# Blocks 5 and 6 of the first MLP computed as a pair with seven products, and attention's last product in fp32

## The chip, the cores and the metric

One core of a Trainium2 chip runs the whole program. Its engines are TensorE (PE; PEld is its weight load), VectorE (DVE), ScalarE (ACT), GpSimd (POOL) and SyncE (SP), which here issues nearly all DMAs. The metric is the device time of one execution in microseconds. Three runs of the kernel before gave 1582.0, 1582.98 and 1583.49; the median is 1582.98.

## What is computed

```python
# attention: q, k, v are (8, 8, 576, 64)
q_s = softmax(q, axis=-1)                       # over the 64 entries of a head
k_s = softmax(k, axis=2)                        # over the 576 positions
kv  = einsum('bhsd,bhse->bhde', k_s, v)         # 64 x 64 for each head
x   = einsum('bhsd,bhde->bhse', q_s, kv)        # 8 x 8 x 576 x 64
x   = x.transpose(0, 2, 1, 3).reshape(4608, 512)
# first MLP: w_in 512 x 2048, w_out 2048 x 512
h = x @ w_in;   x = (h * clip(h + 3, 0, 6) / 6) @ w_out
# second MLP, same shapes
h = x @ w2_in;  return (h / (1 + exp(-h))) @ w2_out
```

## The kernel before

The 4608 tokens are nine blocks of 512 (0 to 8). Every product of an MLP is made of three passes in fp32r (high by high, high by low, low by high), so each operand is held as a high and a low part: a copy on ACT makes the high part, a subtraction on DVE the low part.

**A block by itself** has 16 slices of 128 hidden columns. A slice has 12 matmuls of 512 columns into one bank `h` (`mm1`, L561), the gate on ACT and DVE (`Gate`, L574 to L592), and 12 matmuls into four banks `y` (`mm2`, L633; L635 in the second MLP). A slice is a step. Before, blocks 0 to 6 of the first MLP and block 0 of the second are done so.

**A pair of blocks** is one pass of `second_mlp`: the 2 x 2 scheme with seven products in place of eight. Its first half ("inner", L1345) has 8 rounds of seven products, its second half ("outer", L1504) seven products of 8 rounds; each of the 112 has 6 matmuls. The operands are sums of quarters. Those of the weights lie in DRAM (`ws`, second index: which of the two matrices; first index: which MLP) and are fetched into a ring of six buffers; those of the tokens are made during the pass before (`x_ahead`). `PASSES` lists the passes as (MLP - 1, first block): before it is (1, 1), (0, 7), (1, 3), (1, 5), (1, 7). An inner half also carries the transposes of the results of the pass before (`turn_blocks`), an outer half the splits of the gates (L1450 on ACT, L1332 on DVE; L1332 is a helper that records every `add`).

**Attention** works in 36 units, one for each block and pair of heads. A unit makes `kv` (`kv_mm`, L397, ten fp32 matmuls of 65 columns), turns the normalized q (early units by TensorE, later ones through DRAM: `q_blocks`, `q_store`, `q_load`) and multiplies both (`x_mm`, L515). Before, `x_mm` takes three fp32r products of split operands: `kv_upper`, `kv_lower`, `q_upper`, `q_lower` make the parts. A block of 512 tokens can lie in two batches, and then the product is made in two pieces.

**The weights** arrive in a packed form. `Conv` unpacks a slice (ACT L120, L124; DVE L132, L139, L143). Those of the first MLP stay in SBUF for the single blocks; those of the second are unpacked during the single blocks, split (`Split`, ACT L223, DVE L226), summed in place on POOL (`sums_in_place`, L194), and stored to `ws`. For the pair (0, 7) the same was done with the first MLP's weights (`Resident`).

**The order** of `first_block` (to the end of block 0) and `middle` (the other single blocks) is made by `Plan`: jobs with an engine, an estimated duration, a key (the step that they belong to, shifted by the tables `LATE`, `WORK`, `FETCH`, `UNIT`, `CONV`, `RAW`), dependencies, and buffers taken and given. It plays them against its estimates and writes each engine's instructions in the resulting order; on the chip each engine works through its list strictly in that order. `second_mlp` is ordered by a list of events in units of one product (6 matmuls). SP's list is in order as well: a DMA that waits for its producer holds all behind it.

Of the kernel before, what the change touches and what calls it, by code (L numbers as in the profile page):

```python
# [28 lines left out]
def efficient_attention_then_two_mlps(  # L29
# [24 lines left out]
    NCL = NB - 2  # L54
    FAR = 4
    PASSES = ((1, 1), (0, NCL)) + tuple((1, j) for j in range(3, NB, 2))
# [17 lines left out]
    kvt = [const.tile([P, 2, P], F32R, name=f"kv{i}") for i in range(KVS)]  # L74
# [8 lines left out]
    ws = dram.tile([2, 2, 4 * NF, P, DM], F32, name="ws")  # L83
    xq = dram.tile([NB - FAR, NC, P, BLK], F32, name="xq")
# [118 lines left out]
    def store_parts(ph, o, i, flat, names):  # L203
        for h, name in enumerate(names):
            if name != "A21" or ph:
                nc.sync.dma_start(
                    ws[ph, o, slot(o, i, name)].rearrange("p (a d) -> p a d", a=2),
                    f32(flat)[:, :, h * HALF : (h + 1) * HALF],
                )

    class Split:
# [13 lines left out]
        def lower(self):  # L225
            nc.vector.tensor_tensor(out=self.lo, in0=self.src(), in1=f32(self.hi), op=ALU.subtract)  # L226
# [21 lines left out]
    class Resident:  # L248


        def __init__(self, i, o):
            self.i, self.o = i, o
            self.split = [
                Split(0, o, i, lambda n=n: self.t[:, n], [INTO[x] for x in NAMES[o][n]], False)
                for n in range(2)
            ]
            self.total = [
                lambda m=m: sums_in_place(o, [self.t[:, n] for n in range(2)])[m]() for m in range(4)
            ]

        def flat(self, n):
            f = 2 * self.i + n
            return wo[0, f] if self.o else wi[0, f].rearrange("p a c f -> p a (c f)")

        def whole(self, n):
            if n == 0:
                self.t = raw.tile([P, 2, DM], F32, tag="raw", name="w1_sum")
            w = self.flat(n)
# [140 lines left out]
    def kv_upper(u):  # L409
        pk, rs, t = live["pk", u], live["rs", u], kvt[u % KVS]  # L410
        kv[divmod(u, NP)] = t
        for h in range(2):
            d = slice(h * D, (h + 1) * D)
            nc.scalar.activation(t[d, 0, d], pk[d, 0:D], AF.Copy, scale=rs[d])

    def kv_lower(u):
        pk, rs, t = live.pop(("pk", u)), live.pop(("rs", u)), kvt[u % KVS]
        for h in range(2):
            d = slice(h * D, (h + 1) * D)
            nc.vector.scalar_tensor_tensor(  # L420
                out=t[d, 1, d], in0=pk[d, 0:D], scalar=rs[d], in1=f32(t[d, 0, d]),
                op0=ALU.mult, op1=ALU.subtract,
            )
# [60 lines left out]
    def q_load(u):  # L484
        t = tmp.tile([P, NCH * P], F32, tag="t2k", name="qt")
# [7 lines left out]
    def q_upper(u):  # L493
        qT = att.tile([P, 2, NCH, P], F32R, tag="qT", bufs=1, name="qT")
        nc.scalar.copy(qT[:, 0].rearrange("p i n -> p (i n)"), live["pq", u])
        live["qT", u] = qT

    def q_lower(u):
        qT = live["qT", u]
        nc.vector.tensor_tensor(  # L500
            out=qT[:, 1].rearrange("p i n -> p (i n)"),
            in0=live.pop(("pq", u)),
            in1=f32(qT[:, 0]).rearrange("p i n -> p (i n)"),
            op=ALU.subtract,
        )

    def x_mm(u):
        j, pr = divmod(u, NP)
        qT = live.pop(("qT", u))
        px = a_psum(None)  # L510
        pv = px.rearrange("p (i n) -> p i n", i=NCH)
        for p0, n, b, _ in parts(j):
            w = kv[b, pr]
            for n_, (a, c) in enumerate(((0, 0), (0, 1), (1, 0))):
                nc.tensor.matmul(  # L515
                    pv[:, :, p0 : p0 + n], w[:, a, :], qT[:, c, :, p0 : p0 + n],
                    start=(n_ == 0 and p0 == 0), stop=(n_ == 2), skip_group_check=True,
                )
        live["px", u] = px

    def x_upper(u):
        j, pr = divmod(u, NP)
        if j >= FAR:
            t = live["xq", u] = tmp.tile([P, BLK], F32, tag="t2k", name="xq")
# [208 lines left out]
    class Plan:  # L733
# [84 lines left out]
    LATE = (0, 0, 1.5, 1, 1, 1, 0, 0, -1.5, 0.5, 0.5, 0.5, 0, 0, 0, 0, 0, 0, 0, 0, -1, 2, 0, 0, 3,  # L818
        1.5, 0.5, 2.5)
    WORK = (-2, 0, 0, 0, 0.5, -0.5, 0, -1.5, 0.5, 2.5, 2, 2, 0, 4, 2, 2)  # L820
    FETCH = (2, 0, 0, 0, 0, -0.5, -0.5, -1, -1, -0.5, -2, -1)

    UNIT = (0, -1.5, -1.5, 1.5, 2, 2, 2, 2, 4)
    CONV = (0, 1.5, 1.5, 1.5, 1, 1, 1.5, 1.5, 1, 0.5, 0, -0.5, -1, 0.5, 0, 0, -0.5, 0, -1, -1, 0,
        0.5, 0, -0.5, -1, 2, 0, 1, 0.5, 0.5, 0, 1)
    RAW = (-0.5, 0, 0, 0, 2, 0, 1, 0.5, -2, -2, -2, 0, 0, 0, 0, 0, 0, 0, -2, -1, -1, 1, 0, 0, 0, 0,
        2, 0, -0.5, -2, -2, -2)


    DIRECT_X = ()  # L830
    DIRECT_G = ()
# [888 lines left out]
```

## Time and profile before

| | |
|---|---|
| median of three runs | 1582.98 us |
| profiled execution | 1584.67 us |
| its span, first to last instruction | 1583.0 us |
| PE, PEld, DVE, ACT, POOL busy | 98%, 81%, 72%, 49%, 31% |
| HBM read, written | 247.20 MB, 94.11 MB |
| SP's queue, share of the 16 DMA engines | 69.3% |

The span falls into four parts: up to about 31 us loads and the first units of attention; then the single blocks of the first MLP to 726 us; five passes to 1490.5 us; block 0 of the second MLP to the end. A matmul's record covers its way through the engine, and the records overlap, so a PE busy of 98% isn't work at full rate. The pace is read from the starts: from one run of matmuls to the next.

### The profile page before, as it was taken

How to read it: one execution, taken by the hardware profiler on the slowest of the kernel's cores; microseconds unless marked ns; L12 is line 12 of the kernel's file. 1: busy time of each engine (PE TensorE's matmuls, PEld its weight loads, DVE VectorE, ACT ScalarE, POOL GpSimd, SP SyncE). 2: the span in 40 equal slices, each digit the busy share in tenths (PEclk: the TensorE clock that was granted, in tenths of full speed). 3: DMA queues.
4: the chain of work that ended last, by engine and by line, in shares of the span. 5: the costliest groups of instructions: out<-in, count | busy, mean ns of one | idle time of the engine just before them, and what ended most of it. 6: DMA issues, size and time to landing. Idle time of an engine off the chain costs nothing.

```text
span 1583.0 us, 22655 instructions
## 1 busy us (share of the span) xinstructions
PE 1555.3 (98%) x7388; PEld 1274.9 (81%) x7388; DVE 1146.3 (72%) x1888; ACT 775.1 (49%) x1390; POOL 490.8 (31%) x443
## 2 busy tenths in 40 slices
PE   5999999999999999999999999999999999999998
PEld 3777888887878888888888888888888888888887
DVE  7898567777777787675689569946986697676632
ACT  5787345555555555454355336523543464345322
POOL 3234233334243344632223233223223422440000
PEclk9999999999999999999999999999999999999999
DMA  9914977777777775857566786765667875879840
GB/s 271 332 37 131 321 214 209 204 232 223 238 206 214 228 236 191 255 173 243 197 217 224 206 230 222 256 211 193 234 206 216 222 252 191 225 229 365 259 127 27
DMA packets 391206, 342.85 MB, mean 217 GB/s; under 512 B 184880, under 2 KB 297520, under 8 KB 391088
## 3 DMA queue, kind: packets, MB, share of 16 engines
q1 hardware_dynamic: 389040, 340.32, 69.3%
q8 instruction: 59, 0.97, 0.2%
q10 hardware_dynamic: 2048, 1.08, 0.2%
q14 instruction: 59, 0.48, 0.1%
HBM read 247.20 MB, written 94.11 MB: 216 GB/s over the span
## 4 chain that ended last, share of the span: by engine, by line
PE 93%; DVE 3%; DMA 1%; ACT 1%; issue 1%; SPq 0%; POOL 0%; ACTq 0%; DVEq 0%; POOLq 0%
PE pb L1345 24%; PE pb L1504 24%; PE h L561 21%; PE y L633 17%; PE y L635 3%; PE pa L515 2%; PE pa L397 1%; DVE fa L139 1%; DMA yd<-o 0%; DVE fa L143 0%; DVE fa L132 0%; DVE h L598 0%; DMA wi_early<-in_moe_w_in_dram 0%; DMA ws<-fa 0%; PE pa L368 0%
## 5 line engine op out<-in xcount | busy, mean ns | idle before, releaser
L561 PE MATMUL h<-x,wi 128*128 128x512 f32 x1536 | 382.2, 396 | 1.8 <-ACT g L609 1.4
L1345 PE MATMUL pb<-xo,ring 128*128 128x512 f32 x1680 | 382.6, 389 | 0.0
L1504 PE MATMUL pb<-gsp,ring 128*128 128x512 f32 x1680 | 382.4, 389 | 0.0
L1345 PEld LDWEIGHTS pb<-xo,ring 128*128 128x128 f32 x1680 | 315.3, 188 | 65.5
L1504 PEld LDWEIGHTS pb<-gsp,ring 128*128 128x128 f32 x1680 | 315.3, 188 | 65.5
L561 PEld LDWEIGHTS h<-x,wi 128*128 128x128 f32 x1536 | 285.4, 189 | 63.7 <-ACT g L609 2.2
L633 PE MATMUL y<-g,wo 128*128 128x512 f32 x1344 | 324.6, 391 | 0.7 <-DVE o L652 0.7
L633 PEld LDWEIGHTS y<-g,wo 128*128 128x128 f32 x1344 | 251.0, 188 | 53.7 <-DVE o L652 1.1
L1332 DVE TENSOR_TENSOR gsp<-g,gsp 128x512 fp32r<-128x512 f32 x240 | 182.5, 780 | 25.4 <-ACT gsp L1450 24.7
L1450 ACT CAST gsp<-g 128x512 fp32r<-128x512 f32 x240 | 143.7, 622 | 106.7 <-PE pb L1504 89.4
L574 ACT ACTIVATE r<-h 128x512 f32<-128x512 f32 x112 | 67.0, 598 | 172.4 <-PE h L561 169.9
L598 DVE SCALAR_TENSOR_TENSOR h<-r,h 128x512 f32<-128x512 f32 x112 | 77.5, 692 | 82.6 <-ACT r L574 82.0
L1332 POOL TENSOR_TENSOR xst<-xst 128x512 f32<-128x512 f32 x32 | 71.5, 2235 | 167.5 <-DVE xo L1332 87.1
L1332 DVE TENSOR_TENSOR g<-r,pb 128x512 f32<-128x512 f32 x96 | 65.7, 684 | 54.6 <-ACT r L1359 54.1
L1359 ACT ACTIVATE r<-pb 128x512 f32<-128x512 f32 x96 | 57.1, 594 | 97.2 <-DVE pb L1332 72.8
L1332 POOL TENSOR_TENSOR g<-g 128x512 f32<-128x512 f32 x40 | 53.5, 1338 | 138.2 <-DVE g L1332 113.0
L1332 POOL TENSOR_TENSOR s<-U,s 128x512 f32<-128x512 f32 x32 | 42.3, 1321 | 174.0 <-DVE U L1332 174.0
L589 ACT CAST g<-h 128x512 fp32r<-128x512 f32 x112 | 65.5, 585 | 46.2 <-DVE h L598 38.5
L436 POOL TENSOR_TENSOR qe<-qraw,qm 128x512 f32<-128x512 f32 x34 | 40.2, 1181 | 152.3 <-DVE qz L478 130.2
L592 DVE TENSOR_TENSOR g<-h,g 128x512 fp32r<-128x512 f32 x96 | 66.0, 688 | 21.1 <-ACT g L589 19.8
L1332 DVE TENSOR_TENSOR U<-pb,s 128x512 f32<-128x512 f32 x80 | 55.0, 688 | 17.4 <-PE pb L1345 12.5
L194 POOL TENSOR_TENSOR fa<-fa 128x256 f32<-128x256 f32 x64 | 49.5, 774 | 55.9 <-DVE sp L226 47.8
(161 smaller groups left out, 1778.7 us busy)
## 6 DMA issues: line engine op xcount, KB each, us to landing
ring<-ws SPq DMA_DIRECT2D x280, 512.0 KB, 3.9
ws<-sp SPq DMA_DIRECT2D x256, 128.0 KB, 2.2
wi_early<-in_moe_w_in_dram SPq DMA_DIRECT2D x16, 512.0 KB, 8.7
wo_early<-in_moe_w_out_dram SPq DMA_DIRECT2D x16, 512.0 KB, 8.9
wi_raw<-in_moe_w_in_dram SPq DMA_DIRECT2D x16, 512.0 KB, 5.0
ws<-w_sum SPq DMA_DIRECT2D x64, 128.0 KB, 2.2
ws<-fa SPq DMA_DIRECT2D x64, 128.0 KB, 1.8
wo_raw<-in_moe_w_out_dram SPq DMA_DIRECT2D x16, 512.0 KB, 4.3
```

The source lines that it names most:

```text
L194: lambda to=to, x=x, y=y, op=op: nc.gpsimd.tensor_tensor(out=at[to], in0=at[x], in1=at[y], op=op)
L561: nc.tensor.matmul(h, w[:, a, c, :], x[:, e, c, :], start=(c == 0 and n == 0), stop=(c == NC - 1 and n == 2),)
L574: nc.scalar.activation(self.r, self.h, AF.Relu, bias=3.0)
L589: nc.scalar.copy(self.g[:, 0], self.r)
L592: nc.vector.tensor_tensor(out=self.g[:, 1], in0=self.r, in1=f32(self.g[:, 0]), op=ALU.subtract)
L598: nc.vector.scalar_tensor_tensor(out=self.h, in0=self.r, scalar=6.0, in1=self.h, op0=ALU.min, op1=ALU.mult)
L633: nc.tensor.matmul(y[c], w[:, a, cs], g[:, e, :], start=st, stop=sp)
L1332: (eng or nc.vector).tensor_tensor(out=out, in0=a, in1=b, op=how)
L1345: nc.tensor.matmul(to, ws_[:, a], e[:, c], start=p in ("P1", "P6", "P5") and c == 0 and m == 0, stop=c == 1 and m == 2, skip_group_check=True,
L1359: nc.scalar.activation(r, d[b, n, key], AF.Sigmoid)
L1450: nc.scalar.copy(t[0], source(p, i))
L1504: nc.tensor.matmul(d[b, p][m], w[:, a, m * P : (m + 1) * P], t[e], start=new and i == 0 and k == 0, stop=i == NPR - 1 and k == 2, skip_gro ...
```

## The change

Two more blocks, 5 and 6, leave the single blocks (`NCL` is `NB - 4`) and become the pass (0, 5). The passes are now (1, 1), (1, 3), (0, 5), (0, 7), (1, 5), (1, 7). The stores of the first MLP's plain quarters move from `middle` into `first_block` (`store_first`); in `middle` only the fp32 sum of high and low part is made (POOL) and stored whole (`wf`), and its sums of quarters and splits are made in the inner halves of the first three passes (`first_forms`). `x_mm` is one fp32 product. Some `Split.lower` go to POOL (`ASIDE_P`), four `x_lower` and one gate of `first_block` go from TensorE and ACT to DVE (`DIRECT_X`, `DIRECT_G`), a sum in the inner halves of the second and third pass goes from POOL to DVE (`c22`). The last three units load q and make `x_mm` in the first pass. The tables of the planner are new.

```diff
-    NCL = NB - 2
+    NCL = NB - 4
-    PASSES = ((1, 1), (0, NCL)) + tuple((1, j) for j in range(3, NB, 2))
+    PASSES = ((1, 1), (1, 3), (0, 5), (0, 7), (1, 5), (1, 7))
...
         def whole(self, n):
+            f = 2 * self.i + n
             if n == 0:
                 self.t = raw.tile([P, 2, DM], F32, tag="raw", name="w1_sum")
...
-        def store(self, n):
-            store_parts(0, self.o, self.i, self.flat(n), NAMES[self.o][n])
+        def store(self):
+            nc.sync.dma_start(wf[self.o, self.i], self.t)
...
-    def kv_lower(u):
...
-            nc.scalar.activation(t[d, 0, d], pk[d, 0:D], AF.Copy, scale=rs[d])
+            nc.scalar.activation(t[d, d], pk[d, 0:D], AF.Copy, scale=rs[d])
...
-    def q_lower(u):
...
+    def x_mm(u, pool=lambda: a_psum(None)):
...
         for p0, n, b, _ in parts(j):
-            w = kv[b, pr]
-            for n_, (a, c) in enumerate(((0, 0), (0, 1), (1, 0))):
-                nc.tensor.matmul(
-                    pv[:, :, p0 : p0 + n], w[:, a, :], qT[:, c, :, p0 : p0 + n],
-                    start=(n_ == 0 and p0 == 0), stop=(n_ == 2), skip_group_check=True,
-                )
+            nc.tensor.matmul(
+                pv[:, :, p0 : p0 + n], kv[b, pr], qt[:, :, p0 : p0 + n],
+                start=p0 == 0, stop=True, skip_group_check=True,
+            )
...
-            begin[j * NP + pr] = 3 * pr if j == 1 else NF - 3 + int(3.3 * n) + LATE[n]
+            begin[j * NP + pr] = 3 * pr if j == 1 else NF - 3 + 2.3 * n + LATE[n]
...
-            at = NF + 5.5 * k + 6 + WORK[k]
+            at = NF + 3.7 * k + 4 + WORK[k]
...
-                    nc.gpsimd if b else nc.vector,
+                    nc.gpsimd if b > 2 else nc.vector,
...
+        def first_forms(k, t):
+            o, i = divmod(k, NPR)
+            st = {}
...
+            def high(n):
...
+                nc.scalar.copy(st[n][:, 0], st["t"][n])
+            def low(n):
+                add(st[n][:, 1], st["t"][n], f32(st[n][:, 0]), ALU.subtract)
+            def store(n):
+                for h, x in enumerate(NAMES[o][n]):
+                    nc.sync.dma_start(
+                        ws[0, o, slot(o, i, INTO[x])].rearrange("p (a d) -> p a d", a=2),
+                        f32(st[n])[:, :, h * HALF : (h + 1) * HALF],
+                    )
+            when(t, load)
+            for m in range(4):
+                when(t + 5.8 + 0.6 * m, lambda m=m: sums_in_place(o, st["t"])[m]())
+            for n in range(2):
+                when(t + 12.0 + 0.8 * n, lambda n=n: high(n))
+                when(t + 12.6 + 0.8 * n, lambda n=n: low(n))
+                when(t + 14.0 + 0.8 * n, lambda n=n: store(n))
...
+            for n, k in enumerate(range(5 * b, min(5 * b + 5 + b // 2, 2 * NPR)) if b < 3 else ()):
+                first_forms(k, t0 + (9.0 if b == 0 else 1.2) + (6.6 if b != 1 else 7.2) * n)
...
+        for n, u in enumerate(range(LATER, NB * NP)):
...
+            when(0.1 + 0.1 * n, lambda u=u, to=q_to: q_load(u, to))
+            when(4.97 + n, lambda u=u: x_mm(u, bank))
+            when(6.05 + n, lambda u=u, to=x_to: (x_upper(u, to), x_store(u)))
```

What moves is shown at three places. The first is ACT's list from its first copy for attention on, a few instructions into the program (`qT` or `qt` is the turned q, `x` the block's operand, `fa` and `fr` the unpacking of weights). Before:

```order
L495 CAST qT<-pa 128x512
L414 ACTIVATE kv_94<-pk,small 64x64 x2
L446 ACTIVATE qe<-qe 128x512
L414 ACTIVATE kv_93<-pk,small 64x64 x2
L120 ACTIVATE fa<-wi_early 128x512
L124 ACTIVATE fr<-wi_early 128x512
L495 CAST qT<-pa 128x512
L529 CAST x<-pa 128x512
```

and of the changed kernel:

```order
L479 COPY qt<-pa 128x512
L430 ACTIVATE qe<-qe 128x512
L407 ACTIVATE kv_94<-pk,small 64x64 x2
L502 CAST x<-pa 128x512
L430 ACTIVATE qe<-qe 128x512
L522 CAST x<-pa 128x512
L121 ACTIVATE fa<-wi_early 128x512
L125 ACTIVATE fr<-wi_early 128x512
```

Both copies of the first unit's result `x` and one more exponential now stand ahead of the first weight's unpacking.

The second is SP's list in the middle of the single blocks (`ws` holds the weights' quarters and sums, `zd` and `qt` the way of q through DRAM, `xq` the results of attention for later blocks). Before:

```order
L232 DMA ws<-sp 128x256
L232 DMA ws<-w_sum 128x256
L105 DMA wi_raw<-in_moe_w_in_dram 128x4x256
L482 DMA zd<-qz 128x512
L676 DMA xq<-xq 128x512
L322 DMA qraw<-in_q_dram 80x2x256
L322 DMA qraw<-in_q_dram 48x2x256
L232 DMA ws<-sp 128x256 x4
L488 DMA qt<-zd 32x16x32 x4
```

and of the changed kernel:

```order
L255 DMA wf<-w_sum 128x1024
L466 DMA zd<-qz 128x512
L225 DMA ws<-sp 128x256 x4
L315 DMA qraw<-in_q_dram 96x2x256
L315 DMA qraw<-in_q_dram 32x2x256
L100 DMA wo_raw<-in_moe_w_out_dram 128x1024 x2
L472 DMA qt<-zd 32x16x32 x4
```

The first MLP's weights leave by one DMA in place of eight small ones and three of plain quarters; the rest of the list stays and stands closer. In all of `middle` SP issues 635 DMAs (256 `ws<-sp` and `ws<-fa`, 96 `qt<-zd`, 69 `vbuf`, 214 others), before 821 (384 to `ws` from `sp`, `fa` and `w_sum`, 108, 66, 263 others).

The third is TensorE's list at the start of the first pass (`y` is the last single block's output, `pb` the pass's banks). Before:

```order
L633 MATMUL y_6943<-g,wo 128x512
L633 MATMUL y_6944<-g,wo 128x512
L1345 MATMUL pb<-xo,ring 128x512 x318
L1504 MATMUL pb<-gsp,ring 128x512 x6
L1345 MATMUL pb<-xo,ring 128x512 x6
L1504 MATMUL pb<-gsp,ring 128x512 x330
```

and of the changed kernel:

```order
L1326 MATMUL pb<-xo,ring 128x512 x18
L488 MATMUL pb<-qt,kv_97 128x512
L1326 MATMUL pb<-xo,ring 128x512 x6
L488 MATMUL pb<-qt,kv_93 128x512
L1326 MATMUL pb<-xo,ring 128x512 x6
L488 MATMUL pb<-qt,kv_94 128x512
L1326 MATMUL pb<-xo,ring 128x512 x288
L1485 MATMUL pb<-gsp,ring 128x512 x6
```

Attention's last three products now stand among the first pass's matmuls, each as one fp32 matmul.

## Rows read from the trace of the kernel before

**Rows 1.** Page: busy time of the engine that the program is built around.

```profile
PE 1555.3 (98%) x7388; PEld 1274.9 (81%) x7388; DVE 1146.3 (72%) x1888; ACT 775.1 (49%) x1390; POOL 490.8 (31%) x443
```

**Rows 2.** Page: the chain that ended last, shares of the span.

```profile
PE 93%; DVE 3%; DMA 1%; ACT 1%; issue 1%; SPq 0%; POOL 0%; ACTq 0%; DVEq 0%; POOLq 0%
```

**Rows 3.** Busy time by stage: stretch, length, PE PEld DVE ACT POOL, clock, DMA, GB/s.

```profile
0.00:31.00 31.00, 16.70 (x96) 10.49 (x97) 22.67 (x62) 15.38 (x29) 11.36 (x23) 1.00 0.90 265
31.00:124.00 93.00, 86.94 (x434) 67.81 (x433) 83.87 (x154) 77.04 (x144) 28.96 (x25) 0.96 0.56 188
124.00:726.10 602.10, 600.12 (x3106) 491.78 (x3105) 445.31 (x807) 312.31 (x569) 229.80 (x252) 1.00 0.72 218
881.20:1033.50 152.30, 152.30 (x674) 126.11 (x673) 116.52 (x169) 70.23 (x124) 49.47 (x32) 1.00 0.76 231
```

**Rows 4.** Chain in order of time, two stretches: start, length, what, number.

```profile
204.87 2.72 PE h L561 x12
806.54 5.67 PE pb L1504 x25
```

**Rows 5.** Page: the groups of matmuls that the change removes or adds.

```profile
L561 PE MATMUL h<-x,wi 128*128 128x512 f32 x1536 | 382.2, 396 | 1.8 <-ACT g L609 1.4
L1345 PE MATMUL pb<-xo,ring 128*128 128x512 f32 x1680 | 382.6, 389 | 0.0
L1504 PE MATMUL pb<-gsp,ring 128*128 128x512 f32 x1680 | 382.4, 389 | 0.0
L633 PE MATMUL y<-g,wo 128*128 128x512 f32 x1344 | 324.6, 391 | 0.7 <-DVE o L652 0.7
```

**Rows 6.** TensorE in order of time: a unit's products; start, length to last end.

```profile
233.71 1.03 PE L515 MATMUL pa<-qT,kv 128*128 128x128 f32 x6
234.58 1.78 PE L633 MATMUL y<-g,wo 128*128 128x512 f32 x7
...
621.44 1.03 PE L515 MATMUL pa<-qT,kv 128*128 128x448 f32 x6
622.40 0.95 PE L397 MATMUL pa<-vbuf,ke 128*64 128x65 f32 x20
623.28 1.20 PE L633 MATMUL y<-g,wo 128*128 128x512 f32 x4
```

**Rows 7.** ScalarE in order of time near the start, with its idle time.

```profile
20.40 0.66 ACT L120 ACTIVATE fa<-wi_early 128x512 f32<-128x512 f32 x1 [3.56 <-DMA wi_early<-in_moe_w_in_dram]
```

**Rows 8.** Lines of SP's DMA issues: ns min/median/max of one, first and last start.

```profile
L232 SPq DMA_DIRECT2D ws<-sp x256: 319/442/1982, 159.6 to 726.5; - x128
L488 SPq DMA_DIRECT2D qt<-zd x108: 557/634/1368, 201.4 to 691.7; - x108
L307 SPq DMA_DIRECT2D vbuf<-in_v_dram x58: 565/597/1528, 4.5 to 593.2; - x58
```

**Rows 9.** SP in order of time while the matmuls of rows 4 ran.

```profile
205.30 0.45 SPq L232 DMA_DIRECT2D ws<-sp  x1
205.80 0.45 SPq L232 DMA_DIRECT2D ws<-fa  x1
206.35 0.40 SPq L232 DMA_DIRECT2D ws<-sp  x1
```

**Rows 10.** Waits of SP, 124 to 726 us: total, times, longest.

```profile
SPq L296 <- DVE ke L377: 23.8, 8, 8.1
SPq L232 <- ACT sp L223: 19.2, 10, 5.4
```

**Rows 11.** Waits of TensorE, 124 to 726 us, the largest.

```profile
PE y L633 <- DVE o L652: 0.7, 1, 0.7
```

**Rows 12.** The second pass's inner and outer half, columns as in rows 3.

```profile
881.20:957.30 76.10, 76.10 (x337) 63.04 (x336) 48.11 (x73) 27.27 (x49) 27.78 (x22) 1.00 0.81 221
957.30:1033.50 76.20, 76.20 (x338) 63.06 (x337) 68.41 (x97) 42.96 (x75) 21.69 (x11) 1.00 0.71 242
```

**Rows 13.** DVE's split of weights and POOL's sums: ns min/median/max of one.

```profile
L226 DVE TENSOR_TENSOR sp<-fa,sp x32: 640/690/1626, 152.5 to 713.2; 128x512 fp32r<-128x512 f32 x32
```

More of the change, by code (lines that the diff above doesn't have):

```diff
@@ L885, in unit @@
             qt_ = add("PE", 0.65, key(3), lambda: q_turn(u), [qn], ["a"], [qe])
-            qu = add("ACT", 0.6, key(3), lambda: q_upper(u), [qt_], ["qT"])
-            ql = add("DVE", 0.69, key(3), lambda: q_lower(u), [qu], [], ["a"])
+            ql = add("ACT", 0.6, key(3), lambda: q_copy(u), [qt_], ["qT"], ["a"])
             pkb = f"y{u}" if small else "a"
@@ L964, in first_block @@
         last = None
-        done = {}
+        stores = [(f, o) for f in range(NF) for o in range(2)]
         for f in range(NF):
@@ L973, in first_block @@
                 )
+            for _ in range(4 if f >= 6 else 0):
+                if stores:
+                    i, o = stores.pop(0)
+                    k = 1 if i % 2 != o else 2
+                    add(
+                        "SP", 0.4 * k, f + 2.0, (lambda i=i, o=o: store_first(i, o), 262144 * k),
+                        [split[o, i], m],
+                    )
             g = Gate(s)
@@ L1036, in unit @@
                 qt_ = add("PE", 0.65, key(3), lambda: q_turn(u), [qn], ["a"], ["qe"])
-                qu = add("ACT", 0.62, key(3), lambda: q_upper(u), [qt_], ["qT"])
-                ql = add("DVE", 0.69, key(3), lambda: q_lower(u), [qu], [], ["a"])
+                ql = add("ACT", 0.62, key(3), lambda: q_copy(u), [qt_], ["qT"], ["a"])
             else:
@@ L1051, in unit @@
                 va = add("DVE", 0.45, key(4), lambda: kv_sum(u), [mm])
-                vu = add("ACT", 0.55, key(4), lambda: kv_upper(u), [va])
-                vlow[u] = add("DVE", 0.6, key(4), lambda: kv_lower(u), [vu], [], ["a"])
+                vlow[u] = add("ACT", 0.55, key(4), lambda: kv_scale(u), [va], [], ["a"])
             xm = xmm[u] = add(
-                "PE", 0.8, key(6), lambda: x_mm(u), [ql, vlow.get(u), vlow.get(u - NP)], ["a"], ["qT"]
+                "PE", 1.0, key(6), lambda: x_mm(u), [ql, vlow.get(u), vlow.get(u - NP)], ["a"],
+                ["qT"] if u < DIRECT else ["qT", "z"],
             )
@@ L1075, in middle, with parted @@
             unit(u)
-        def parted(split, key, deps, give=()):
+        def parted(split, key, deps, give, aside):
             sp = ["sp"] * (1 + split.keep)
             hi = add("ACT", 0.64, key, split.upper, deps, sp)
-            lo = add("DVE", 0.72, key, split.lower, [hi], [], [], True)
+            if aside:
+                lo = add("POOL", 1.2, key, lambda: split.lower(nc.gpsimd), [hi], [], [], True)
+            else:
+                lo = add("DVE", 0.72, key, split.lower, [hi], [], [], True)
             st = dma(1.4, key, split.store, 512, [lo], [], sp + list(give))
@@ L1102, in middle @@
             for n in range(2):
-                parted(p.split[2 + n], at + 1.4 + n, done, ["t2k"])
+                parted(p.split[2 + n], at + 1.4 + n, done, ["t2k"], 4 * k + 2 + n in ASIDE_P)
             w = Resident(i, o)
@@ L1113, in middle @@
                 ]
-            for m, fn in enumerate(w.total):
-                done = [add("POOL", 0.68, at + 2.3 + 0.1 * m, fn, done, [], [], True)]
-            for n in range(2):
-                done.append(parted(w.split[n], at + 2.5, done, ["raw"] if n else []))
+            dma(0.35, at + 2.2, w.store, 512, done, [], ["raw"])
         steps = [(0, j, f) for j in range(NCL) for f in range(NF)]
@@ L1539, in joins, with turn_blocks @@
                 when(t + k, lambda m=m, name=name: do(m, name))
-        turned = []
-        def turn_blocks(j, k, part):
+        turned, gone = [], []
+        def turn_blocks(b, k, part):
+            j = PASSES[b][1]
             h, n = (1, k) if k < NC else (0, k - NC)
@@ L1550, in turn_blocks @@
                 if not turned:
-                    turned.extend(split_tile())
+                    turned.extend(split_tile() if b > 1 else [gone.pop() if k else small("o2")])
+                if b < 2:
+                    gone.append(x)
                 nc.vector.transpose(f32(turned[0]), x)
@@ L1561, in turn_blocks @@
                 turned.pop(0)
-        gone = []
         def turn_last(j, k):
```

137 lines of the change are left out of this document (67 added, 70 removed).

## The prediction, made before the changed kernel had run

> **What bounds the kernel now.** I read the busy times first: TensorE is busy for 98% of the span, no other engine for more than 72% (besides its own weight load) [rows 1]. A busy record can hide a slow pace, so the chain of work that ended last comes next: 93% of it is TensorE [rows 2]. Then the pace, in the chain by time: 12 matmuls of a single block in 2.72 us, 25 of a pass in 5.67 us, 0.2267 us each in both [rows 4]. A pass has 112 products of 6, 672 matmuls, 152.3 us at this pace, and the second pass's stretch is just that long [rows 3]: the passes are TensorE and nothing else. The single blocks of the first MLP have seven times 384 matmuls (half of them in each of L561 and L633 [rows 5], where L561 also has a second-MLP block's 192), 609.4 us. Twelve of these already stand in the first pass. From 31.0 to 726.1 us 606.7 of 695.1 us are theirs, and 88.4 us are attention's products and waits. In this stretch TensorE's largest wait by releaser from 124 us on is 0.7 us [rows 11], so nearly all of it is work too. Only before 124 us do others set the pace: there DVE is busy 83.9 of 93 us and ACT 77.0 [rows 3]. So time goes down as TensorE's work does, unless another engine falls behind in what is left.
>
> **Matmuls.** Two single blocks take 768 with them, a pass brings 672. 96 fewer at 0.2267 us: -21.8 us. The passes' waits for bank and operand are treated below.
>
> **Attention's last product.** Before, three fp32r passes. A whole block: 3 x 0.2267 = 0.68 us. In two pieces it is longer, from the first start to the next instruction's: 128 + 384 columns 0.87 us, 64 + 448 columns 0.96 us [rows 6]. Nine blocks, two whole, two of each of these, three between at about 0.76: mean 0.81. An fp32 product of 512 columns isn't in the trace. The nearest row is `kv_mm`: ten fp32 products of 65 columns show 20 records and take 0.88 us to the next instruction [rows 6]; two run side by side on 64 columns of the array each, so one step is 0.176 us. The lower end: two records of one pass each, 0.45 us. The upper: 0.176 us scaled by 512/65, 1.39 us. Since 0.176 us is six times what 65 columns take in one fp32r pass (0.029 us) and a part of it must be fixed, I take two passes for each record, four times 0.2267, and with second pieces 0.93. 36 units by +0.12: +4.3 us; the ends are -12.9 and +20.9. The last three, now in the first pass, cost there what they no longer cost before.
>
> **The start.** ACT waits 3.56 us for the first weight [rows 7], and the copies for the second unit stand behind it; now three attention instructions stand ahead. In `first_block` seven `q_lower` and eight `kv_lower` leave DVE, four `x_lower` and a gate come: some 3.5 us less on the engine that is 90% busy there. Between nothing and -7 us (both); I take -3. The 40 stores of plain weights that come in late here fall on a DMA share of 0.56 and cost nothing.
>
> **The single blocks that are left.** Here the change makes everything denser: 65 steps in place of 97 carry the same unpacking and 27 of the units. TensorE needs 65 x 5.44 us and about 26 units of 1.8 us (0.93 and 0.88), 401 us. DVE goes by counts and rows from 445 of 602 us to some 325 of 401, 81% for 74%: `q_lower`, `kv_lower` and half of the weight splits pay for most. The queue that gets full is SP's. Its issues take 0.44, 0.63 and 0.60 us [rows 8] with 0.05 to 0.10 us between them [rows 9]. Before: 384, 108, 66 and 263 others at 0.5 (estimated between these rows), 409 us, and 821 gaps of 0.08: 475 of 602 us, 79%. After: 256, 96, 69 and 214 others, 322 us and 51 us: 373 of 401, 93%. The lower end of what this costs is nothing: around 205 us SP issues without a pause [rows 9] and the matmuls beside it run at full pace [rows 4]; loads are keyed two to three steps, 12 to 20 us, ahead of use. The upper end: SP keeps its other 127 us of pauses, which are waits for producers such as [rows 10], in proportion to its DMAs, 98 us, which makes 471 us, 70 more than TensorE needs. What is queued behind a late SP: a weight's load holds ACT's unpacking, a store that hasn't gone holds one of three `sp` buffers, and behind both stand the gates for which TensorE waits. I take a third of the pauses, 33 us, so about 407 us: +7 with rounding, near the lower end, since a late SP finds its producers done.
>
> **The passes.** The first three get 16 sets of sums and splits, and the second and third 8 sums each from POOL to DVE. DVE in an inner half had 48.1 of 76.1 us; 8 x 0.69 and ten to twelve splits at 0.69 [rows 13] make 62. The outer half carries 68.4 of 76.2 without a pause on TensorE [rows 12], and a bank is used again only eight allocations later, some two rounds. So nothing, at most 16 delays of one such instruction, 11 us; I take +1. The last three units' q comes by 12 DMAs at the pass's start, 8.7 us of issue; the third product stands 54 matmuls, 12 us, behind the start. If SP arrives late there TensorE waits: +1, at most some 5.
>
> **A rule against the change.** The split of a weight on DVE takes 640 ns at best and up to 1626 [rows 13]; POOL is busy 230 of 602 us there [rows 3] and would be about 214 of 401. The Trainium skill, page "SBUF — State Buffer", section "SBUF: two separate sides", says that DVE and GpSimd share a pair of ports as an exclusive lock: a DVE instruction with two SBUF inputs and a GpSimd one exclude each other for their whole length. The row agrees with it. By that rule, about 120 such DVE instructions would meet POOL in 53% instead of 38% of cases; it is a rival below.
>
> **Sum.** -21.8 + 4.3 - 3 + 7 + 1 + 1 = -11.5 us. The profiled execution took 1584.7 us, so 1573.2; the median of the runs is 1.7 us below it: 1572 us. Its own range, 1564 to 1580, is the waits of SP between none and half.
>
> **Rivals.**
> SP becomes the bound. More than half of its pauses stay, since each wait in its list holds all DMAs behind it. For: 93% against 79%, and the planner's own costs for an issue (0.35 us) are below every median in [rows 8]. Against: no pause beside [rows 9]. It decides from 373 + 98 x 0.5 = 422 us on, 21 us over TensorE's need, where all gain is gone; at 0.6 of the pauses it is 432 us, 24 us more than in my sum: 1596 us, slower.
> The fp32 product is two passes: 17 us less than my value, 1555 us. For it speaks that there are two records for a product, against it their pace.
> The fp32 product costs as `kv_mm` scaled: 17 us more, 1589 us, slower. Against it: the row is full of short instructions and weight loads.
> The inner halves fall behind: 6 or 7 us of waits in the first three passes, where sums, splits and stores stand between the gates; 1579 us. Against it: [rows 12].
> DVE and POOL exclude each other: 0.15 x 120 meetings at half of a POOL instruction of about 1 us, 9 us more on DVE; if all of it reached TensorE 1581 us, no change. Against it: DVE would still have 67 us free.
> That the change does less than it says is excluded by the order: 4032 matmuls of pairs stand in TensorE's list.
>
> **Chances.** My forecast 0.45, SP 0.20, slow passes 0.13, cheap fp32 0.08, ports 0.08, dear fp32 0.06. A measurement here tells 0.2%, 3.2 us, from no change: faster is below 1579.8, slower above 1586.2. Faster: 0.42 + 0.07 + 0.08 + 0.03 = 0.60 (forecast, passes, cheap fp32, ports); the same: 0.03 + 0.06 + 0.05 + 0.02 = 0.16 (forecast, passes, ports, SP); slower 0.24. The range, 1558 to 1596, leaves out about half of the cheap-fp32 case and the worse half of SP's, some 0.15.
>
> **What would show it.** Passes of 152.3 us, the first 2.8 longer for its three products. An fp32 piece of 512 columns, start to next start, near 0.91 us. The first pass starting near 31 + 432.5 (1908 matmuls) + 88.4 + 4 (fp32) - 2.7 (three products moved) - 3 + 7, 557 us; later than 570 us says that the single blocks lost time, and then ACT waiting for `wi_raw` or `wo_raw`, or POOL and ACT for `ws<-sp`, names SP. I am wrong if TensorE waits more than some 15 us between 124 us and the first pass, or if a pass is over 156 us.

## The result and the profile after

The changed kernel takes 1601.28 us (median of 4 runs, 1599.04 to 1603.67), the kernel before 1583.12 in the same four rounds: a ratio of 1.0114, interval [1.0101, 1.0126]. It is slower, by 1.1%. The forecast was 1572, faster, and the time lies above the range too (1558 to 1596). The page of the profiled execution, the lines that answer to [rows 1, 2]:

```profile
PE 1547.4 (97%) x7223; PEld 1249.7 (78%) x7223; DVE 1170.0 (73%) x1864; ACT 786.5 (49%) x1406; POOL 568.5 (35%) x488
...
PE 65%; DMA 5%; DVE 3%; SPq 2%; ACT 1%; issue 1%; POOL 1%; ACTq 0%; DVEq 0%; POOLq 0%
```

TensorE lost 8 us of busy time and the span grew by 19. In the chain, DMAs have gone from 1% to 5% and SP's issues from nothing to 2%. Where the 30.9 us between forecast (a span of 1571.0) and measurement (1601.9) lie is seen by the starts of the passes. The kernel before has five passes, the changed one six, so the last row starts at the fifth there and at the sixth here:

| us | before | forecast | after |
|---|---|---|---|
| first pass starts | 726.1 | 557 | 566.3 |
| first pass | 155.1 | 158.9 | 173.7 |
| second and third | 152.3 each | 305.6 | 155.1 + 158.1 |
| fourth and fifth | 152.3 (the fourth alone) | 304.6 | 304.6 |
| from the last pass's start | 244.9 | 244.9 | 244.1 |

So 9.3, 14.8 and 7.6 us are lost against the forecast, and nothing behind the third pass. By stage, columns as in [rows 3]: the first block, the other single blocks, then inner and outer half of the first pass and of the second, and the third's inner half:

```profile
31.00:124.00 93.00, 88.54 (x433) 68.14 (x433) 86.87 (x149) 78.57 (x145) 28.99 (x25) 1.00 0.89 306
124.00:566.25 442.25, 426.42 (x2246) 337.12 (x2245) 312.45 (x572) 228.93 (x417) 212.04 (x210) 0.99 0.79 235
566.25:662.40 96.15, 84.92 (x349) 67.35 (x348) 60.96 (x88) 38.55 (x68) 42.09 (x41) 0.93 0.88 297
662.40:739.90 77.50, 77.50 (x343) 64.19 (x342) 69.99 (x101) 43.91 (x77) 21.15 (x10) 1.00 0.65 225
739.90:817.40 77.50, 75.29 (x331) 61.67 (x330) 61.02 (x90) 33.23 (x59) 35.96 (x34) 1.00 0.98 298
817.40:895.10 77.70, 77.66 (x343) 64.30 (x344) 68.09 (x98) 42.87 (x75) 21.04 (x10) 1.00 0.68 237
895.10:975.20 80.10, 77.51 (x331) 62.64 (x330) 60.25 (x90) 32.76 (x59) 39.24 (x38) 0.98 0.99 302
```

An inner half, taken up to the first matmul of the outer one, is 77.5 us without a wait in the first pass (12 matmuls of the last single block stand in it) and 74.8 in the others; an outer half is 77.5. Only inner halves are long, and in those of the second and third pass the DMA share is 0.98 and 0.99, where it was 0.81 before [rows 12]. The head of the first pass, first SP, then TensorE, in order of time:

```profile
569.64 1.91 SPq L225 DMA_DIRECT2D ws<-sp  x4
574.86 0.32 SPq L466 DMA_DIRECT2D zd<-qz  x1
...
579.26 1.97 SPq L1173 DMA_DIRECT2D ring<-ws  x4
581.28 11.04 SPq L472 DMA_DIRECT2D qt<-zd  x12
592.41 0.57 SPq L1173 DMA_DIRECT2D ring<-ws  x1
```

```profile
571.69 1.52 PE L1326 MATMUL pb<-xo,ring 128*128 128x512 f32 x6
574.27 1.65 PE L1326 MATMUL pb<-xo,ring 128*128 128x512 f32 x6 [1.06 <-ACT s L1360]
583.22 2.90 PE L1326 MATMUL pb<-xo,ring 128*128 128x512 f32 x6 [7.29 <-DMA ring<-ws]
588.99 2.05 PE L488 MATMUL pb<-qt,kv 128*128 128x512 f32 x2 [2.88 <-DMA qt<-zd]
590.05 3.55 PE L1326 MATMUL pb<-xo,ring 128*128 128x512 f32 x6
```

The loads of the pass's third to sixth ring slots go out at 579.3, 13 us behind the pass's start; they stand in SP's list behind the last unit's store (`zd`, 574.86) and the last sums' stores. In the kernel before, the same row came 1.9 us behind the start (726.1):

```profile
728.05 2.60 SPq L1192 DMA_DIRECT2D ring<-ws  x5
```

Behind the wait TensorE is slow too: six matmuls take 3.55 us in place of 1.52. Four-microsecond windows of the changed kernel show the granted clock at 0.50, the 1.2 GHz level, after the 7.3 us in which it waited for the ring:

```profile
580.00:584.00 4.00, 0.78 (x2) 0.72 (x3) 0.00 (x0) 0.60 (x1) 0.00 (x0) 0.62 0.89 283
584.00:588.00 4.00, 2.11 (x5) 1.10 (x4) 0.69 (x1) 0.00 (x0) 0.00 (x0) 0.50 1.06 309
588.00:592.00 4.00, 3.01 (x5) 1.81 (x6) 0.92 (x2) 0.92 (x2) 0.00 (x0) 0.50 0.57 89
```

### The profile page after: what moved, and what is told of

Its sections match the earlier page's. It is cut to its first block, busy times and chain, and to the rows that moved or that the text cites. A ratio compares the mean times of both kernels' runs of the same rounds, so it can differ in the third digit from the quotient of the medians.

```text
span 1601.9 us, 22540 instructions
## 1 busy us (share of the span) xinstructions
PE 1547.4 (97%) x7223; PEld 1249.7 (78%) x7223; DVE 1170.0 (73%) x1864; ACT 786.5 (49%) x1406; POOL 568.5 (35%) x488
## 4 chain that ended last, share of the span: by engine, by line
PE 65%; DMA 5%; DVE 3%; SPq 2%; ACT 1%; issue 1%; POOL 1%; ACTq 0%; DVEq 0%; POOLq 0%
PE pb L1485 28%; PE pb L1326 24%; PE h L534 6%; PE y L606 3%; PE y L608 3%; DMA ws<-w1s 2%; DMA xq<-xq 1%; DMA ws<-fa 1%; DMA qt<-zd 1%; PE pa L488 1%; SPq L472 0%; PE pa L390 0%; DMA ring<-ws 0%; DVE g L1349 0%; SPq L225 0%
## 5 line engine op out<-in xcount | busy, mean ns | idle before, releaser
L1326 PE MATMUL pb<-xo,ring 128*128 128x512 f32 x2016 | 467.4, 393 | 11.9 <-DMA ring<-ws 7.6
L1485 PE MATMUL pb<-gsp,ring 128*128 128x512 f32 x2016 | 459.4, 389 | 1.4 <-DMA ring<-ws 1.3
L1326 PEld LDWEIGHTS pb<-xo,ring 128*128 128x128 f32 x2016 | 380.6, 189 | 96.1 <-issue 10.0
L1485 PEld LDWEIGHTS pb<-gsp,ring 128*128 128x128 f32 x2016 | 378.1, 188 | 80.9 <-DMA ring<-ws 1.7
L534 PE MATMUL h<-x,wi 128*128 128x512 f32 x1152 | 293.0, 399 | 5.2 <-DVE g L565 2.0
L534 PEld LDWEIGHTS h<-x,wi 128*128 128x128 f32 x1152 | 212.1, 189 | 53.6 <-DVE g L565 2.8
L1313 DVE TENSOR_TENSOR gsp<-g,gsp 128x512 fp32r<-128x512 f32 x288 | 220.0, 781 | 31.9 <-ACT gsp L1431 30.9
L606 PE MATMUL y<-g,wo 128*128 128x512 f32 x960 | 235.2, 394 | 1.5 <-DVE o L625 1.5
L606 PEld LDWEIGHTS y<-g,wo 128*128 128x128 f32 x960 | 180.1, 189 | 40.8 <-DVE o L625 1.9
L1340 ACT ACTIVATE r<-pb 128x512 f32<-128x512 f32 x96 | 57.2, 596 | 96.3 <-DVE pb L1313 75.2
L1313 POOL TENSOR_TENSOR spare<-g,g 128x512 f32<-128x512 f32 x48 | 65.5, 1365 | 3.7
```

What stands on the lines that cost most here:

```text
L534: nc.tensor.matmul(h, w[:, a, c, :], x[:, e, c, :], start=(c == 0 and n == 0), stop=(c == NC - 1 and n == 2),)
L606: nc.tensor.matmul(y[c], w[:, a, cs], g[:, e, :], start=st, stop=sp)
L1313: (eng or nc.vector).tensor_tensor(out=out, in0=a, in1=b, op=how)
L1326: nc.tensor.matmul(to, ws_[:, a], e[:, c], start=p in ("P1", "P6", "P5") and c == 0 and m == 0, stop=c == 1 and m == 2, skip_group_check=True,
L1340: nc.scalar.activation(r, d[b, n, key], AF.Sigmoid)
L1485: nc.tensor.matmul(d[b, p][m], w[:, a, m * P : (m + 1) * P], t[e], start=new and i == 0 and k == 0, stop=i == NPR - 1 and k == 2, skip_gro ...
```

## The experiments

All are against the kernel before on the same chip, whose median was 1583.7 to 1584.3 in these rounds. "Head" is the inner half of the first pass (96.2 us in the changed kernel, 77.5 + 2.8 without a wait). Starts and heads are read from one profiled execution each: e15 has e5's single blocks and starts its first pass 2.9 us later, so a difference of 1 or 2 us between them says nothing. The kernels of e1, e2, e6, e11, e14 and e16 leave out a part of the work or store it in wrong places; their times show what that part costs.

**SP's issues (e1, e5, e6).** Theory: SP's list is late. Rival: the DMA engines' bytes.

```diff
-            for h, name in enumerate(self.names):               # four of 128 KB
-                to = ws[self.ph, self.o, slot(self.o, self.i, name)]
-                for a, t in enumerate((self.hi, self.lo)):
-                    nc.sync.dma_start(
-                        to[:, a * HALF : (a + 1) * HALF], f32(t)[:, h * HALF : (h + 1) * HALF]
-                    )
+            for name, t in zip(self.names, (self.hi, self.lo)): # e1: two of 256 KB
+                nc.sync.dma_start(ws[self.ph, self.o, slot(self.o, self.i, name)], f32(t))
+                nc.sync.dma_start(wx[len(extra)], f32(t)[:, 0:8])  # e6 alone: 4 KB more each
...
```

> The changed kernel with each split's four stores of 128 KB made two of 256 KB (same bytes, 128 issues fewer on SP's queue in the single blocks; the parts land in other slots than they should, so the products of the pairs are not the reference's). If SP's queue is what is late: SP has some 58 us less to issue before the first pass, the first pass starts 6 to 10 us earlier than in the changed kernel (566 us) and most of the 18.7 us that its inner half lost goes too, since the loads of the ring no longer stand behind late stores: about 1580 us. If the DMA engines' bytes are the bound: the same within 3 us, 1601 us.

Measured: 1583.75, ratio 1.000 [0.9991, 1.001]; first pass from 549.0, head 93.5. The single blocks have won 17 us with the same bytes, more than the 6 to 10 expected; the head has kept most of its loss, against the expectation.

e5 writes to the right slots, both with one DMA for a high or low part: `to = ws[ph, o, s0 : s1 : s1 - s0]`, rearranged to `p h d`.

> The changed kernel with each split's four stores of 128 KB made two of 256 KB that write both parts to their right slots (each row of 2 KB goes as two pieces of 1 KB, as before). If it is the number of SP's issues that counts: nearly as e1, where the rows went in one piece: first pass from about 550 us, total 1584 us, somewhat more if such an issue takes 0.6 us in place of 0.39. If e1 gained by its longer pieces, no gain here: 566 us, 1600 us.

Measured: 1584.46, ratio 1.0007 [0.9996, 1.0018]; first pass from 551.0, head 93.4. So e1 did not gain by its longer pieces: e5 has the changed kernel's bytes and pieces and 128 issues fewer.

> e1's two stores of 256 KB for each split, and beside each a store of 4 KB to a place that nobody reads, so that SP issues as many DMAs as in the changed kernel (the parts land in wrong slots, as in e1). If SP's issues are the bound: most of e1's 17 us are lost again, less what a small issue is shorter by: first pass from 557 to 565 us, total 1591 to 1600 us. If bytes or pieces are: as e1, 549 us and 1584 us.

Measured: 1601.97, ratio 1.0112 [1.0097, 1.0127]; first pass from 568.4. All of the gain is gone. The issue durations on SP, ns min/median/max, of the changed kernel's stores, of e5's, and of e6's large and small ones:

```profile
L225 SPq DMA_DIRECT2D ws<-sp x192: 319/448/1674, 145.4 to 578.2; - x192
```

```profile
L226 SPq DMA_DIRECT2D ws<-sp x96: 359/427/1977, 146.3 to 560.7; - x96
```

```profile
L225 SPq DMA_DIRECT2D ws<-sp x96: 319/413/2002, 146.7 to 578.9; - x96
...
L226 SPq DMA_DIRECT2D wx<-sp x96: 320/437/1567, 147.2 to 579.4; - x96
```

128 KB, 256 KB and 4 KB cost the same to issue. The single blocks as a whole, first e1, then e6 (columns as in [rows 3]):

```profile
124.00:549.00 425.00, 421.40 (x2252) 336.56 (x2252) 314.30 (x574) 230.38 (x421) 213.39 (x211) 1.00 0.80 245
```

```profile
124.00:568.40 444.40, 428.36 (x2252) 338.36 (x2251) 313.10 (x574) 230.61 (x420) 212.31 (x211) 0.99 0.80 236
```

The same 2252 matmuls and the same work on DVE, ACT and POOL, 19.4 us apart, at a DMA share of 0.80 in both. With e5 this shows it: it is the number of issues, not the bytes or the pieces.

**The same in the kernel before (e9).** e5's edit there.

> The kernel before with e5's merged stores: two DMAs of 256 KB for each split in place of four of 128 KB, 128 issues fewer. If SP became the bound only through the change (79% loaded before, 93% after by the prediction's count), nothing is gained here: 1582 to 1584 us. If SP's queue costs time at any load, some 10 us are gained.

Measured: 1581.14, ratio 0.998 [0.9971, 0.9989]: 3 us, first pass from 723.8. A small miss: by this, SP's queue already cost a little at 79%. This version beats both kernels.

**The first MLP's sums in the passes (e2, e11, e16).** e2 and e11 leave out `first_forms`, e16 only its stores (e11 and e16 on e10, below). All passes then fetch the second MLP's weights, which the second pass does in every kernel:

```diff
-                first_forms(k, t0 + (9.0 if b == 0 else 1.2) + (6.6 if b != 1 else 7.2) * n)  # e2, e11
...
-                when(t + 14.0 + 0.8 * n, lambda n=n: store(n))  # e16
...
-            ws[PASSES[b][0], o, 2 * m : 2 * m + 2].rearrange("s p d -> p s d"),
+            ws[1, o, 2 * m : 2 * m + 2].rearrange("s p d -> p s d"),
```

> The changed kernel without the sums and splits of the first MLP's weights in the first three passes (left out with their loads and stores; passes three and four take the second MLP's parts in their place). If these bring the DMA engines to their limit in the inner halves: the inner halves of the second and third pass go back to 77.5 us with their 12 matmuls of the pass before (from 77.5 and 80.1, so 3 to 5 us are won), and the first pass keeps its loss, since its ring loads were late before the first of these loads was issued: about 1594 us. If the first pass's loss is theirs too, it falls to 80 us: about 1580 us.

Measured: 1593.89, ratio 1.0066 [1.0049, 1.0083]; inner halves 74.8 in the second and third pass, head 95.1. As expected by the first theory.

> e10 without the sums and splits of the first MLP's weights in the first three passes (left out as in e2). What is then left over the count of matmuls is not theirs: the second and third pass go to 152.3 us, 4 to 6 us less than e10 with what they add to the first pass: 1566 to 1570 us. If they are what delays the head too, 10 us less or more.

Measured: 1571.22, ratio 0.9912 [0.9893, 0.993], 10.7 us under e10, where 4 to 6 were expected; head 87.8. In the profiles 9 us of it lie in the second and third pass.

> e10 with the sums and splits of the first MLP's weights made but not stored (64 DMAs of 256 KB left out; passes three and four take the second MLP's parts, as in e11). If the DMAs cost the passes their time (the buffers that wait for a store's landing, the full DMA engines): the second and third pass go to 152.3 us as in e11, total near 1571 us. If it is the instructions in the lists: as e10, 78 to 79 us in the inner halves, 1581 us.

Measured: 1571.65, ratio 0.992 [0.9904, 0.9937]. The second pass's inner half in e10, e11 and e16:

```profile
719.90:798.80 78.90, 76.94 (x332) 62.90 (x331) 58.77 (x88) 33.42 (x59) 35.20 (x34) 0.98 1.00 297
```

```profile
717.60:792.40 74.80, 74.80 (x331) 61.96 (x331) 51.06 (x78) 28.56 (x49) 18.08 (x14) 1.00 0.83 220
```

```profile
720.80:795.60 74.80, 74.80 (x331) 61.94 (x330) 59.78 (x92) 34.26 (x62) 35.68 (x34) 1.00 0.86 250
```

e16 has DVE's, ACT's and POOL's work of e10 and the time of e11: the instructions cost nothing, the 64 stores cost 10 us, at a DMA share of 1.00 with them and 0.86 without. In the changed kernel ScalarE waits for their landing in the third pass's inner half, and they land late, 5.3 us (median) behind their issue, where 256 KB of the kernel before took 3.0:

```profile
ACT w1s L1581 <- DMA ws<-w1s: 6.6, 2, 3.4
...
ws<-w1s SPq DMA_DIRECT2D x64, 256.0 KB, 5.3
...
ws<-wi SPq DMA_DIRECT2D x24, 256.0 KB, 3.0
```

The first two lines are the changed kernel's, the last is the kernel before's. A store holds its buffer until it has landed, and `w1s` shares its buffers with the gates. Whether more buffers would have hidden the late landings was not run: e16 takes away the bytes and the held buffers together.

**POOL's splits (e4).** `ASIDE_P = ()`.

> The changed kernel with the 30 splits of weights that POOL does before the first pass given back to DVE. If POOL is what makes the stores late (its sums and splits stand right before the stores that hold SP at the start of the first pass): the first pass starts up to 5 us earlier and its ring wait shrinks: 1590 us. If DVE's load matters more, or the planner's order, no gain: 1600 to 1606 us.

Measured: 1603.55, ratio 1.0129 [1.0113, 1.0145]; first pass from 571.4, head 92.0: what the head wins, the start loses. POOL's splits are not what costs the time.

The ports' rival can't be judged by the median of DVE's split (684 ns with POOL's splits, 682 without). The trace shows the exclusion. In the kernel before, 64 of the 96 splits on DVE had no POOL instruction beside them and took at most 694 ns; 21 took 906 to 1626 ns, and each of these ended 546 to 551 ns behind the end of a POOL instruction that ran when it began, as here (POOL's ends at 347.54, DVE's at 348.08):

```profile
346.23 1.31 POOL L462 TENSOR_TENSOR qe<-qe,qs 128x512 f32<-128x512 f32 x1 [1.43 <-DVE qs L458]
...
346.55 1.53 DVE L226 TENSOR_TENSOR w_sum<-w_sum,sp 128x512 fp32r<-128x512 f32 x1
```

But it costs no more than before: from 31 us to the first pass, DVE's instructions that ended so lost some 35 us in the kernel before, 35 in the changed kernel and 37 in e4 (an estimate: each one's time over the median of its kind with POOL idle). The 9 us more that the rival has are not there.

**The head: other lists (e3, e7, e8).** e3 issues the ring's loads 2 to 5 from ScalarE; e7 also 6 to 9 and one q load, and puts the three products later (and the first pass's sums by 1.6 products, as do all the runs below with late products); e8 is e7 with e5.

```diff
-            fetch(k)
+            fetch(k, nc.scalar)                             # e3, e7
...
-            when(4.97 + n, lambda u=u: x_mm(u, bank))
...
+            q_at, x_at = ((0.3, 8.97), (4.0, 15.47), (8.0, 16.97))[n]   # e7
...
+            when(x_at, lambda u=u: x_mm(u, bank))           # e7
```

> The changed kernel with the four first loads of the ring (slots 2 to 5) issued from ScalarE's queue in place of SP's. If SP's order is the cause (these loads stand behind eight to sixteen stores that wait for POOL and for DVE): TensorE's wait of 7.3 us for the ring in the first pass goes, and part of the low clock behind it; the inner half of the first pass falls from 96 to about 85 us, the total to about 1590 us. If the DMA engines are full there, the loads land as late from either queue: 1600 us.

Measured: 1601.31, ratio 1.0109 [1.009, 1.0128]; head 96.3. The ring's wait went, and TensorE waited 10.5 us for q instead: the expectation failed.

> The changed kernel with only the head of the first pass changed: the ring's loads 2 to 9 and the q load of the first of the three late units from ScalarE's queue, so that none stands behind the last unit's store, and the three products later (9, 15.5 and 17 products into the pass in place of 5 to 7). If the 18.7 us are lost because ring and q stand behind a chain of the last unit and the last sums (POOL, then DVE, then SP), the inner half of the first pass falls from 96 to 82 us or so with no low clock: 1587 us. If only the order of the same lateness changes, as in e3, it stays over 92 us.

Measured: 1602.8, ratio 1.0115 [1.01, 1.013]; head 96.4: failed.

> e5 and e7 together. The two causes are apart if their gains add: first pass from 550 us and its inner half near 82 us: 1570 us, faster than before by 13 us. If the head of the pass only waits for what SP brings late, the second gain is smaller: 1578 us or more.

Measured: 1589.28, ratio 1.0029 [1.0019, 1.0039]; head 95.8: failed. ScalarE in order of time in e8 shows why:

```profile
555.28 0.62 ACT L216 CAST sp<-fa 128x512 fp32r<-128x512 f32 x1 [4.49 <-POOL fa L195]
...
556.10 1.96 ACTq L1175 DMA_DIRECT2D ring<-ws  x4
558.10 9.15 ACTq L474 DMA_DIRECT2D qt<-zd  x4
567.29 0.58 ACT L1362 COPY s<-pb 128x512 f32<-128x512 f32 x1 [10.58 <-DMA qt<-zd]
```

Its list has the last sums' splits ahead of the pass too, so the ring still goes out 6.4 us behind the pass's start (549.7); and four q loads behind 2 MB of ring loads held the issuing engine for 9 us, with the pass's copies behind them.

**The head: order and load (e10, e12 to e15).** e10 is e5 with the ring's first loads and one q load as jobs of the planner, ahead of the last stores on SP, and late products; e15 is e5 with late products alone. Where products come later, a part of the loss moves into the outer half, so the first pass as a whole is given beside the head; it is 171.0 us in e5 and 157.9 without a wait.

```diff
+            ("r2", "SP", 0.35, 11.0, rest(0), 512, ("r1",), ["x"], False),   # e10, and r3 to r5
...
+                    dma(1.4, key(4), lambda: q_load(u), 256, [z0], ["qT", "z"])   # e10, u == LATER
```

> e5's merged stores, and the head of the first pass in another way than in e7 and e8: nothing goes to ScalarE's queue; the four first loads of the ring and the q load of the first late unit stand in the planner's list, so ahead of the last stores on SP; the three products of the late units come 9, 15.5 and 18 products into the pass. If e7 and e8 kept the loss only because ScalarE's own list (behind POOL's last sums, and with q's issue held behind 2 MB of the ring's loads) took SP's place, the first pass's inner half falls from 93 to 80 to 84 us: total 1571 to 1575 us. If the loss is the last unit's chain itself, on which TensorE waits whatever the order, it stays over 90 us: 1583 us.

Measured: 1581.9, ratio 0.9988 [0.9979, 0.9997]; head 89.4, the pass 168.1. Of the 13.1 us that e5's head loses, 4 are won, some 3 in the pass as a whole; that is neither theory's figure. The longest wait of TensorE is now for ScalarE:

```profile
562.37 11.08 PE L1337 MATMUL pb<-xo,ring 128*128 128x512 f32 x36 [3.73 <-ACT s L1371]
```

> e5 with only the three late products moved to 9, 15.5 and 17 products into the first pass and their q loads spread behind the first loads of the ring, all on SP. If these loads and products are their own part of the head (e13 against e12: 5 us less in the inner half), the inner half falls from 93.4 to 87 to 89 us, 1579 us. If the lists' late end is all of it: 92 us or more, 1584 us.

Measured: 1586.74, ratio 1.0015 [1.0004, 1.0026]; head 91.9, but the pass takes 171.0 as in e5: late products alone win nothing, the list's late end is what costs.

Three theories were left: (a) the lists of the single blocks are so ordered that SP, ScalarE and the last unit's chain end behind TensorE; (b) the four last sums on POOL hold the rest; (c) the late units' q loads do. e14 leaves these sums out of e5.

> e5 without the four sums on POOL of the last set of the second MLP's weights (left out; their splits store the plain parts). By theory (b) these 4 us of POOL and the wait of ScalarE's and SP's lists on them hold the head: inner half from 93 to 87 us or less, 1577 us. By (a) the last unit's chain still ends late: 91 us or more, 1581 us or more.

Measured: 1584.77, ratio 1.0001 [0.9991, 1.0011]; head 91.7, the pass 169.2: not the last sums alone.

e12 and e13 have new tables (`LATE`, `WORK`, `FETCH`, `ASIDE_P`) and costs in the planner (a merged store 0.95, a q load 2.6, a sum on POOL 0.98 and so on); e13 the late products too.

> e5 with another order of the single blocks: the planner's costs for SP's issues and POOL's instructions set to the durations measured in the changed kernel's trace, and its tables of due times chosen anew so that in its list TensorE, ScalarE and SP end closer together (the first pass as in the changed kernel). By theory (a) both the first pass starts earlier than e5's 551 us (540 to 548) and its inner half loses less (from 93 to 85 to 89, with the late q loads still in the way): about 1570 us. If only the q loads hold the head (c): the inner half stays at 93 us, 1576 us. If such tables move nothing on the chip: 1584 us.

Measured: 1597.15, ratio 1.0082 [1.0066, 1.0097]; first pass from 568.2, head 89.2, the pass 166.8. The single blocks were expected to end earlier than e5's and end 17 us later: failed.

> e12 with the three late products 9, 15.5 and 17 products into the first pass and their q loads spread behind the first loads of the ring. By theory (a) with the lists in order this takes the rest of the head: inner half 80 to 83 us, 1563 to 1568 us. By (c) the same gain should show here, 10 us less than e12; if the three products and their loads do not matter, e12's time.

Measured: 1593.95, ratio 1.0061 [1.0046, 1.0076]; first pass from 568.1, head 84.3, 9 us less than e5's, the pass 163.2, some 8 less. The head of e13:

```profile
573.58 2.88 PE L1334 MATMUL pb<-xo,ring 128*128 128x512 f32 x12
577.79 7.09 PE L1334 MATMUL pb<-xo,ring 128*128 128x512 f32 x30 [1.33 <-DMA ring<-ws]
...
597.62 1.02 PE L490 MATMUL pb<-qt,kv 128*128 128x512 f32 x2
598.08 1.96 PE L1334 MATMUL pb<-xo,ring 128*128 128x512 f32 x6
599.88 1.02 PE L490 MATMUL pb<-qt,kv 128*128 128x512 f32 x2
```

The waits at the head are nearly gone, but the single blocks end 17 us later than in e5: what the head had lost is lost before it. This fits theory (a), by which the head is the tail of the single blocks' work, but e12 and e13 changed many things at once; that a better order exists which ends both early is not shown.

## Why the prediction was wrong

**Matmuls: right.** Three passes take exactly 152.3 us, and with SP relieved the first pass starts at 549 to 551 (e1, e5), where the forecast without its term for SP has 550.

**Attention's last product: right, the size a little high.** From a whole fp32 product to the next 2.26 us pass in e13 (rows above), six matmuls (1.36) and 0.90: two passes for each of the two records, as taken. Pieces, counted from the unit's start to the fourth matmul behind it less four times 0.2267: 128 + 384 columns 0.89 in both kernels, 192 + 320 columns 0.88 for 0.80, 64 + 448 columns 0.99 for 0.97; whole 0.90 for 0.72. About +2.6 us over the 36 units in place of +4.3. Both fp32 rivals are out.

**The start: right in kind, the size low.** The 600th of the MLPs' own matmuls starts at 192.4, before at 198.1, with as many units of attention done: 5.8 us for 3, inside its range of 0 to 7.

**"I take a third of the pauses": failed.** The count was good: SP's issues and the gaps between them fill 329 + 39 us from 124 us to the first pass (forecast 373). But SP paused for 58.5 us (gaps of over 0.15 us), not 33; with 15 us of its semaphore instructions that is the whole stretch of 442 us. This is 0.6 of the 98 us of the upper end, which I had as the rival's number. The reason given, that a late SP finds its producers done, failed. SP's waits from 124 us to the first pass are many and short, and the largest are:

```profile
SPq L225 <- ACT sp L216: 6.7, 4, 2.4
SPq L300 <- PE pa L390: 6.5, 3, 3.7
SPq L472 <- PE pa L390: 5.0, 2, 4.1
```

That behind each late producer the next DMAs come late for others fits a list in order, but is argued, not shown. The cost is 16 us over the 550 for +7. By my own figures it should have been more: 432 us at 0.6 of the pauses, 31 over the 401 that TensorE needs. But the 401 were too low: with SP relieved (e1), 411 us pass from the 385th matmul of the MLPs, with which the 65 steps begin, to the first pass. So the two errors cancel in part.

**"The passes ... So nothing, I take +1": failed.** I counted DVE and POOL, and for these e16 shows nothing lost. The DMA engines were left out. They were in the rows: a share of 0.81 at 221 GB/s in an inner half [rows 12], to which five or six sets add 1 MB of stores each, some 70 GB/s, and half as much of loads; scaled by the stores alone, a share of 1.07. The second and third pass lost 8.6 us; by e11 and e16 it is the stores.

**"The third product stands 54 matmuls, 12 us, behind the start": failed**, the largest miss. It takes for granted that SP is through with the single blocks when the pass starts, as before (1.9 us behind). It is 13 us behind, with the ring's loads, which I didn't price, ahead of q; TensorE waits 7.3 us for the ring and 2.9 for q. The chain to these loads runs through POOL's last four sums (569.0 to 573.1), POOL's and DVE's last instructions for the last unit (to 574.9), its store and eight more on SP. Without the sums the ring goes out 7.8 us behind the pass's start (e14), with them 10.7 (e15): they are a part, and the rest stays open. The same work of unpacking and splitting 32 weights and of attention, in 65 steps for 97, ends after TensorE's last matmul on SP, POOL and ScalarE; e3, e7 and e8 show that another list does not help. Order gives 3 to 8 us of the first pass back in e10, e12 and e13, the last two at 17 us more before it, and nothing in e15. Part of the loss is the clock at its lower level behind the wait.

**The rivals.** SP as the bound was the right one for the single blocks: to relieve it wins 17 us (e1, e5, e6), of which 7 stood in the forecast, so it explains some 10 of the 29 us between forecast and measurement. "The inner halves fall behind" was right in place and price (6 or 7 us for 8.6), for another reason. That DVE and POOL exclude each other is true in the traces, but cost no more than before (e4). The cases were priced as if they excluded each other, and three losses came together: SP's issues, SP's list that goes on into the first pass, and the stores. Of the signs, TensorE stood idle for 15.8 us from 124 us to the first pass (the mark was 15), and the third pass took 158.1 us (the mark was 156). With merged stores, a better head and without the work of `first_forms` (e11), the program takes 1571, with 8 us of the head left. That this is near the forecast is luck: it leaves work out. How to win these losses with the work done is open.

## What to carry to other kernels

Where a change removes matmuls but not the work beside them, count for each in-order list, the DMA queue's own too, when it ends the stage against when TensorE does, and price what the next stage finds still queued. An issue cost SP some 0.43 us here for 4, 128 or 256 KB, so count issues and merge stores first where SP's list is near full. Add up the DMA share by stage: in the changed kernel a mean of 0.75 hid stages at 0.98 to 1.00.

## What the runs showed of the hardware

An issue on SP takes the same for 4, 128 and 256 KB (medians 0.437, 0.448, 0.427 us). Behind 2 MB of loads on a queue four issues of q loads held the issuing engine for 9.15 us (e8), where the median of one is 0.634. A whole fp32 product of 512 columns costs 0.90 us, no more than 0.18 over three fp32r products. In the kernel before, 21 of 96 splits on DVE took 0.9 us or more, and each ended some 0.55 us behind a POOL instruction that ran when it began; the 64 with no POOL instruction beside them took at most 0.694.
